# Block-sparse attention and a gated feed-forward on one core: attention values with queries on the output partitions, a ones column in V, batch 0 turned on TensorE, and a list-scheduled program order

## The chip, the cores and the metric

The kernel runs on one core of one Trainium2 chip. The metric is device time in microseconds (us) of one execution. Engines are called as in the profile: PE is TensorE (PEld its weight loads), DVE is VectorE, ACT is ScalarE, POOL is GpSimd, SP is SyncE (SPq, POOLq: their queues, which issue DMAs).

The profile records one execution. Its span, from first to last instruction, is given beside the times: 389.4 us for the kernel before, whose median time is 386.9 us. That profiled run was the slowest of its four (389.81 us), so about 3 us of any difference in spans to it are its own.

## The reference, cut to what matters

```
q, k, v: (4, 8, 768, 64) float32        # batch, heads, sequence, head width
scores = q @ k^T / 8, masked by blocks of 32: neighbours, first and last
         block row and column, and 3 sampled blocks per block row
attn   = softmax(scores);  a = attn @ v
x      = a as (3072, 512)               # 4*768 tokens, 8*64 features
out    = (sigmoid(x @ w_gate) * (x @ w_val)) @ w_out    # 512 -> 1536 -> 512
```

All the work is dense: the kernel computes every score and multiplies the exponentials by a 0/1 mask.

## The kernel before: the parts that matter

Scores are made transposed, with keys on the partitions and queries along the free dimension. A *unit* is one score tile: 256 keys by 256 queries for a pair of heads. There are 144 units, three to a *pair* (256 queries of two heads over all 768 keys), so 48 pairs. Values then have V as the stationary operand. The row sums come from extra matmuls with a block of ones; their reciprocals are spread over the partitions by another matmul.

```
def values(n, p):                       # cut
    t = ps.tile([128, 512], f32, tag="pvz", bufs=1)
    for j in range(NJ):                 # 6 key blocks of 128
        for hd in range(2):
            nc.tensor.matmul(t[hd*64 : hd*64+64, 0:CH], v_[:, hd, j, :],
                pts[j//2][:, hd, (j%2)*CH : (j%2+1)*CH], ...)      # 64 weight columns, 256 wide
    for j in range(NJ):
        for half in range(2):
            for hd in range(2):
                nc.tensor.matmul(t[r0 : r0+32, CH : CH+128], ones, ...)   # row sums, 24 of them
def recips(n, p):  nc.vector.reciprocal(rz, pvz[n, p][:, CH : CH+128])    # 128x128
def unnorm(n, p):  nc.scalar.copy(xu, pvz.pop((n, p))[:, 0:CH])
def spread(n, p):  # two matmuls sel x rz -> rb (PSUM)
def norm(n, p):    nc.vector.tensor_tensor(xT[g, p][...], xu, rb, op=ALU.mult)
```

The order is written by hand. Queries and keys of batch 0 are turned by DMA, and one loop issues two units a step; the feed-forward of a group of 512 tokens begins 16 steps after its attention.

```
for p in range(NP):
    cast_qk(0, p)                       # f32 -> f16 on DVE and ACT
    transpose_qk(0, p)                  # nc.sync.dma_start_transpose
    ...
for s in range(last + 1):
    mine = units[2*s : 2*s+2]
    fi = s - 12 - LAG                   # LAG = 4
    for u in mine: scores(*u)
    if pv_now: values(*pv_now)
    if g is not None: ffn_in(g, f, wg, pgs)
    ... exps, masks, recips, tanhs, unnorm, ffn_in(g, f, wv, pvs), gates, spread, norm, ffn_out
```

The weights are loaded by POOL's queue with a cast to f16, and they are issued from 4.2 us on, right after V of batch 0.

The softmax here doesn't subtract the row's maximum and nothing guards it: scores larger than these inputs give would overflow.

## Time and profile before

| | before |
|---|---|
| median time | 386.89 us (4 runs, 386.20 to 389.81) |
| span of the profiled run | 389.4 us |
| first score matmul | 36.2 us |
| first feed-forward matmul | 94.7 us |
| last matmul ends | 385.5 us |
| PE busy, 0–62 us | 17.4 us |
| PE busy, 150–300 us | 144.4 us, at granted clock 1.00 |

These lines are from the profile page of the kernel before: busy time of the engines; then the span in 40 slices, PE's busy share and the granted clock, in tenths; then the chain of work that ended last, by engine and by line.

```profile
PE 321.1 (82%) x3284; PEld 161.7 (42%) x3284; DVE 226.9 (58%) x359; ACT 197.9 (51%) x269; POOL 40.8 (10%) x53
...
PE   2002277678999999999999999999999999999975
...
PEclk9999996857999999999999999999999999999999
...
PE 68%; ACT 13%; DMA 8%; DVE 4%; issue 4%; SPq 3%; ACTq 0%
PE gv L290 25%; PE py L317 16%; PE pvz L222 11%; ACT pt L203 8%; PE st L192 8%; PE pvz L235 6%; DMA kT<-k_153 4%; DMA ks<-in_k_dram 4%; ACT tg L301 3%; DVE rz L251 2%; SPq L114 2%; PE rb L263 2%; ACT xu L256 1%; DVE y L327 1%; SPq L85 1%
```

PE is the bound from slice 11 on, but it is mostly idle in the first five slices (49 us), and the clock drops in slices 7 to 10. The timeline shows what the start waits for (start us, duration us, queue or engine, line, operation, what it writes and reads):

```profile
20.57 5.05 SPq L114 DMA_TRANSPOSE kT<-k_133  x1
25.71 4.74 SPq L114 DMA_TRANSPOSE qT<-q_151  x1
30.54 4.80 SPq L114 DMA_TRANSPOSE kT<-k_153  x1
...
36.16 1.04 PE L192 MATMUL st<-qT,kT 64*128 64x256 f16 x8 [28.05 <-DMA kT<-k_133]
...
48.26 1.37 SPq L114 DMA_TRANSPOSE kT<-k_169  x1
```

The bracket is PE's idle time before the first scores and what ended it: a DMA transpose that was issued at 20.57 us and landed at 36.1 us.

The next lines are the steady part, in PE's timeline. Each line starts before the one ahead of it has ended, so what one line costs is the distance from its start to the next start.

```profile
206.17 0.61 PE L192 MATMUL st<-qT,kT 64*128 64x256 f16 x8
206.71 0.85 PE L222 MATMUL pvz<-pt,v_1183 128*64 128x256 f16 x12
207.49 0.52 PE L235 MATMUL pvz<-pt,ones 128*32 128x128 f16 x24
207.94 0.39 PE L290 MATMUL gv<-x_1712,wg 128*128 128x512 f16 x1
```

Twelve value matmuls cost 0.78 us and 24 ones matmuls 0.45 us, so 1.23 us a pair. These are the groups that the change removes (count, busy us, mean ns of one, idle before):

```profile
L251 DVE RECIPROCAL rz<-pvz 128x128 f16<-128x128 f32 x48 | 45.7, 952 | 8.1 <-PE pvz L235 8.0
L235 PE MATMUL pvz<-pt,ones 128*32 128x128 f16 x1152 | 27.0, 234 | 0.0
...
L263 PE MATMUL rb<-rz,sel 128*128 128x128 f16 x96 | 13.4, 221 | 9.4 <-ACT tg L301 8.5
```

**A yardstick used throughout: the PE time that a kernel needs.** It is each matmul's count times its spacing at full clock, read from the timelines, plus 0.1 us for each change into or out of the scores' 64-row mode. The last point is where the trace agrees with the Trainium skill, "TensorEngine Tiling (Array Packing)", Key Properties, which says that a change of tiling mode drains TensorE: the last 512-wide matmul before scores is followed after 0.312 us instead of 0.2155 us. For the kernel before:

| part | count x spacing | us |
|---|---|---|
| feed-forward, 512 wide | 864 x 0.2155 | 186.2 |
| scores | 576 x 0.0538 | 31.0 |
| values | 576 x 0.065 | 37.4 |
| ones | 1152 x 0.01875 | 21.6 |
| spreads | 96 x 0.056 | 5.4 |
| block mask | | 2.1 |
| mode changes | 144 x 0.1 | 14.4 |
| sum | | 298.1 |

The span less this sum, 91 us, is called *idle* below. It contains waits, the time before the first and after the last matmul, and what a lower granted clock costs.

### The profile page before, as it was taken

Reading aid. Unit: us, or ns where it says so; the run is one execution under the profiler, and the core shown is the slowest. Engines: PE = TensorE matmul, PEld = TensorE weight load, DVE = VectorE, ACT = ScalarE, POOL = GpSimd, SP = SyncE. Lnnn points to the kernel's source line nnn. Section 1 sums busy time; section 2 is a strip of 40 time slices with the busy share of each in tenths; the row PEclk is TensorE's granted clock in tenths of the full one; section 3 lists DMA queues with packets and bytes.
Section 4 is the critical chain, followed back from the end, with each engine's and each line's share of the span. In section 5 each row is a group of like instructions: output and inputs, shape, how many; then the busy total and the mean of one; then the engine's idle time right before and its main releaser. Section 6 shows DMA issues by size and latency. Waiting matters only on the chain.

```text
span 389.4 us, 7801 instructions
## 1 busy us (share of the span) xinstructions
PE 321.1 (82%) x3284; PEld 161.7 (42%) x3284; DVE 226.9 (58%) x359; ACT 197.9 (51%) x269; POOL 40.8 (10%) x53
## 2 busy tenths in 40 slices
PE   2002277678999999999999999999999999999975
PEld 0001044444555544454444444444444454444432
DVE  5100366677887766767676667676667666432321
ACT  1111256776777766665666566656666564222200
POOL 7200022213220001102020201000000000000000
PEclk9999996857999999999999999999999999999999
DMA  8999988665770003223442450400000000010012
GB/s 186 271 169 195 195 187 194 139 177 85 149 135 2 2 3 108 50 42 112 90 119 51 134 145 12 57 29 29 6 25 27 29 2 29 28 54 29 28 54 81
DMA packets 47151, 33.64 MB, mean 86 GB/s; under 512 B 26996, under 2 KB 44044, under 8 KB 47116
## 3 DMA queue, kind: packets, MB, share of 16 engines
q1 hardware_dynamic: 38012, 25.28, 25.0%
q0 software_dynamic: 9104, 7.87, 14.1%
q8 instruction: 25, 0.41, 0.5%
q14 instruction: 10, 0.08, 0.1%
HBM read 28.42 MB, written 6.29 MB: 89 GB/s over the span
## 4 chain that ended last, share of the span: by engine, by line
PE 68%; ACT 13%; DMA 8%; DVE 4%; issue 4%; SPq 3%; ACTq 0%
PE gv L290 25%; PE py L317 16%; PE pvz L222 11%; ACT pt L203 8%; PE st L192 8%; PE pvz L235 6%; DMA kT<-k_153 4%; DMA ks<-in_k_dram 4%; ACT tg L301 3%; DVE rz L251 2%; SPq L114 2%; PE rb L263 2%; ACT xu L256 1%; DVE y L327 1%; SPq L85 1%
## 5 line engine op out<-in xcount | busy, mean ns | idle before, releaser
L203 ACT ACTIVATE pt<-st 128x1024 f16<-128x1024 f32 x144 | 139.3, 1024 | 83.9 <-PE st L192 83.8
L209 DVE TENSOR_TENSOR pt<-pt,mask 128x1024 f16<-128x1024 f16 x144 | 99.1, 688 | 91.4 <-ACT pt L203 91.4
L192 PE MATMUL st<-qT,kT 64*128 64x256 f16 x576 | 49.5, 292 | 39.0 <-DMA kT<-k_133 28.0
L301 ACT ACTIVATE tg<-gv 128x512 f32<-128x512 f32 x72 | 43.1, 599 | 51.5 <-PE gv L290 49.5
L192 PEld LDWEIGHTS <-kT 64*128 64x128 f16 x576 | 23.7, 98 | 67.0 <-issue 29.1
L251 DVE RECIPROCAL rz<-pvz 128x128 f16<-128x128 f32 x48 | 45.7, 952 | 8.1 <-PE pvz L235 8.0
L290 PEld LDWEIGHTS <-wv 128*128 128x128 f16 x288 | 28.2, 98 | 34.3 <-issue 0.5
L290 PEld LDWEIGHTS <-wg 128*128 128x128 f16 x288 | 23.8, 98 | 29.1 <-issue 4.0
L235 PE MATMUL pvz<-pt,ones 128*32 128x128 f16 x1152 | 27.0, 234 | 0.0
L256 ACT COPY xu<-pvz 128x256 f32<-128x256 f32 x48 | 17.7, 368 | 15.8 <-DVE rz L251 15.7
L327 DVE TENSOR_SCALAR y<-py 128x512 f32<-128x512 f32 x24 | 16.6, 691 | 11.8 <-PE py L317 11.4
L235 PEld LDWEIGHTS <-ones 128*32 128x32 f16 x1152 | 18.0, 102 | 10.9 <-issue 10.9
L263 PE MATMUL rb<-rz,sel 128*128 128x128 f16 x96 | 13.4, 221 | 9.4 <-ACT tg L301 8.5
L263 PEld LDWEIGHTS <-sel 128*128 128x128 f16 x96 | 8.8, 97 | 24.3 <-issue 19.4
L171 PE MATMUL pm<-mb_125,e_70 24*128 24x256 f16 x18 | 4.8, 401 | 4.8 <-DVE mask L178 3.8
L178 DVE CAST mask<-pm 128x512 f16<-128x512 f32 x9 | 5.9, 687 | 0.2
L106 POOL CAST q_2129<-qs 128x768 f16<-128x768 f32 x1 | 0.8, 822 | 43.2 <-issue 43.2
L171 PEld LDWEIGHTS <-e_70 24*128 24x128 f16 x18 | 2.1, 125 | 7.7 <-issue 7.1
L222 PE MATMUL pvz<-pt,v_82 128*64 128x256 f16 x36 | 3.8, 358 | 1.8 <-ACT xu L256 1.8
L104 ACT CAST k_133<-ks 128x768 f16<-128x768 f32 x1 | 0.8, 832 | 8.6 <-DMA ks<-in_k_dram 8.6
L290 PE MATMUL gv<-x_354,wg 128*128 128x512 f16 x12 | 4.6, 386 | 0.5 <-DVE h_1325 L306 0.2
L290 PE MATMUL gv<-x_952,wg 128*128 128x512 f16 x12 | 4.7, 389 | 0.1
(385 smaller groups left out, 540.5 us busy)
## 6 DMA issues: line engine op xcount, KB each, us to landing
qs<-in_q_dram SPq DMA_DIRECT2D x16, 384.0 KB, 3.8
ks<-in_k_dram SPq DMA_DIRECT2D x16, 384.0 KB, 5.2
out_dram<-y SPq DMA_DIRECT2D x24, 256.0 KB, 2.0
wg<-in_moe_w_gate_dram POOLq DMA_DIRECT2D x3, 512.0 KB, 22.8
wv<-in_moe_w_val_dram POOLq DMA_DIRECT2D x3, 512.0 KB, 25.4
wo<-in_moe_w_out_dram POOLq DMA_DIRECT2D x3, 512.0 KB, 30.2
v_76<-in_v_dram POOLq DMA_DIRECT2D x1, 192.0 KB, 3.7
v_82<-in_v_dram POOLq DMA_DIRECT2D x1, 192.0 KB, 6.8
```

The lines of the kernel that those rows point to most:

```text
L192: nc.tensor.matmul(st[:, hd, jj * CH : (jj + 1) * CH], kT[r, j, :], qT[r, 2 * c : 2 * c + 2, :], start=True, stop=True,)
L203: nc.scalar.activation(pt, sts.pop((n, p, tt)), AF.Exp, scale=SCALE)
L209: nc.vector.tensor_tensor(pt, pt, m.unsqueeze(1).to_broadcast([128, 2, 512]), op=ALU.mult)
L222: nc.tensor.matmul(t[hd * 64 : hd * 64 + 64, 0:CH], v_[:, hd, j, :], pts[j // 2][:, hd, (j % 2) * CH : (j % 2 + 1) * CH], start=(j == 0), ...
L235: nc.tensor.matmul(t[r0 : r0 + 32, CH : CH + 128], ones, pts[j // 2][:, hd, o : o + 128], start=False, stop=(j == NJ - 1), skip_group_chec ...
L251: nc.vector.reciprocal(rz, pvz[n, p][:, CH : CH + 128])
L256: nc.scalar.copy(xu, pvz.pop((n, p))[:, 0:CH])
L263: nc.tensor.matmul(rb[:, half * 128 : half * 128 + 128], sel[:, half, :], rz, start=True, stop=True,)
L290: nc.tensor.matmul(t, w[:, i, f * 128 : (f + 1) * 128], xT[g, i], start=(i == 0), stop=(i == NP - 1),)
L301: nc.scalar.activation(t, pgs.pop((g, f)), AF.Tanh, scale=0.5)
L317: nc.tensor.matmul(pys[g, tt], hts[g, f][:, tt * 128 : (tt + 1) * 128], wo[:, f], start=(f == 0), stop=(f == NF - 1),)
L327: nc.vector.tensor_scalar_mul(y, pys.pop((g, tt)), 0.5)
```

## The change

The intent: let the exponentials be the stationary operand, so that queries land on the output partitions; give V a 65th column of ones, so that row sums come with the values; normalise with a per-partition reciprocal; turn the result back with two PE transposes. Batch 0's q and k are turned on PE too. All instructions are described to a small list scheduler with fixed durations, and the program is emitted in the order that it finds. The diff, cut to its core:

```
-            nc.tensor.matmul(t[hd*64 : hd*64+64, 0:CH], v_[:, hd, j, :], pts[...], ...)
-            nc.tensor.matmul(t[r0 : r0+32, CH : CH+128], ones, pts[...], ...)
+        def values():
+            for jq in range(2):
+                for hd in range(2):
+                    for j in range(NJ):
+                        nc.tensor.matmul(
+                            o()[:, 2 * jq + hd, 0:65],
+                            pts[j // 2]()[:, hd, j % 2, jq * 128 : jq * 128 + 128],
+                            v_[:, hd, j, 0:65], start=(j == 0), stop=(j == NJ - 1))
+        P.op("PE", 1.1, values, reads=[*pts, v16[b, p]], writes=[o], prio=seq + 0.1, mode="full")
+        P.op("DVE", 0.15, lambda: nc.vector.reciprocal(rz(), o()[:, :, 64:65]), ...)
+        P.op("DVE", 0.42, ... x16 = o[:, :, 0:64] * rz ...)
+        P.op("PE", 0.12, turn, ...)          # 2 x nc.tensor.transpose, in the same PSUM bank o
+        P.op("ACT", 0.39, ... copy to xT ...)
...
+    def turn_pe(nm, b, p, prio, eng, out_eng):   # batch 0: 6 transposes, then a copy
...
+GROUPS = [[0], [1, 2], [3, 4], [5, 6], [7, 8], [9, 10], [11]]   # feed-forward groups, 256 rows each entry
+LAT = {"PE": 0.35, "ACT": 0.2, "DVE": 0.2, "POOL": 0.25, "SP": 0.1}
+class Plan: ...                               # list scheduler: op(eng, dur, fn, reads, writes, prio)
+    P.run()
-    for s in range(last + 1): ...             # the hand-written order
```

V is now loaded as f32 and cast on POOL (its rows are 66 wide). The weights are loaded in more pieces, and the scheduler places them on POOL's queue after the third cast of V.

## The prediction

> **What bounds it now.** TensorE, after a slow start. By the stretches: 0–62 us has only 17.4 us of PE work, 62–90 us runs at granted clock 0.68, and 150–300 us is 96% busy at clock 1.00. In the timeline the first scores start at 36.2 us (batch 0's eight DMA transposes are issued one behind the other; the chain of waits shows ks, two issues of 4.7 us, then kT 15.6 us), and the feed-forward (FFN) starts only near 98 us, 16 steps later. After that three steps take 13.06 us. The last matmul ends at 385.5 of 389.4 us.
>
> **PE time needed, by pitches in the timeline at full clock** (512-wide matmul 0.2155 us, two score units 0.43 us plus about 0.2 us of row-mode switches, twelve PV matmuls 0.78, 24 ones matmuls 0.45, two spreads 0.11): FFN 864 x 0.2155 = 186; scores 72 x 0.63 = 45; values and ones 48 x 1.23 = 59; spreads 5; masks 3. Sum 298 us.
>
> **Removed:** ones, spreads, the 128x128 reciprocals (952 ns x48), the fp32 copy on ACT (17.7 us), batch 0's DMA transposes.
> **Added:** 24 value matmuls per head pair, 65 columns wide, each with a 128-column weight load; two transposes; a 0.4 us ACT copy; 48 TensorE transposes for batch 0; V casts on POOL.
> The new values depend on weight loads. The Trainium skill ("TensorE: Matmul & The Clock Gate", LDWEIGHTS) gives columns/1.2 ns, 107 ns for 128, but about half with fast weight load. The trace agrees that 128 columns can go faster: the spreads follow each other at 0.055 us, each with its own load. I estimate 46 ns (1.1 us per pair), not over 60 (1.45 us). After: 186 + 45 + 53 + turns 6 + start-up transposes 5 + masks 3 = 298 us. **The PE total does not fall.** The DVE saving (about 35–40 us) and ACT (unchanged, about 200 us) lie off the path.
>
> **What is gained is idle PE time.** Scores should start near 8 us instead of 36, and FFN as soon as weights land. Reads: 3.1 MB of q,k and 1.6 MB of v, then 9.4 MB of weights; at the 200–270 GB/s of the page's early slices the gate/value weights are complete near 42 us (estimate; 40–52). Until then attention runs (ACT and the single o bank hold it to about 1.25 us a unit), some 21 us of PE work plus some 12 of FFN and start-up; then PE is dense: 42 + 265 left + 4% stalls (10) + 4 tail = 321.
>
> **Predicted: 322 us**, range 308 to 342. Faster by over 2%: 0.97; within: 0.02; slower: 0.01.
>
> **What would show it.** First score at 7–10 us; FFN group 0 beginning at 25–40 us; PE about 95% busy from 45 us on; values at 1.1 us a pair; FFN pitch unchanged; DVE near 195 us; so almost all of the gain falls before 100 us, and a few us in the steady state (0.47 us waits for a gv bank vanish).
>
> **What would make it wrong.** Values at 60 ns or over (+17 us); weights later than 52 us; a low clock in the attention-only stretch; the static order, planned with fixed durations (exp 0.93 us where the trace has 0.97 to 1.02), meeting waits on in-order engines: one o bank shared by values and turn, two gv banks; POOL's casts holding back later batches; the 256-wide last group bound by latency (+5 us).

## The result, and the profile after

| | before | after |
|---|---|---|
| median time (4 runs each) | 386.89 us | 321.12 us (319.05 to 322.38) |
| ratio | | 0.8279, 95% interval 0.8232 to 0.8327 |
| span of the profiled run | 389.4 | 320.6 |
| first score / first feed-forward matmul | 36.2 / 94.7 us | 11.7 / 36.9 us |
| PE time needed | 298.1 | 282.1 |
| idle (span less needed) | 91 | 38 |

Ratios are the mean time of one kernel's fast runs over that of the other's fast runs of the same rounds, so they are not quite the ratio of the medians quoted. A control of the changed kernel in a later session (`after_again`) gave 322.13 us and 0.8355.

The total was predicted to within 1 us. The profile shows that two of its terms were not. First the page of the changed kernel, the same rows as before:

```profile
PE 299.2 (93%) x2852; PEld 160.1 (50%) x2852; DVE 204.1 (64%) x374; ACT 196.2 (61%) x279; POOL 51.8 (16%) x69
...
PE   1888898989999999999999999999999999999994
...
PEclk9995999999999999999999999999999999999999
...
PE 69%; ACT 5%; DVE 3%; issue 1%; DVEq 0%; ACTq 0%
PE gv L525 33%; PE py L556 19%; PE o L476 8%; PE st L444 7%; ACT pt L454 4%; PE o L500 1%; DVE h L545 1%; ACT tg L540 1%; DVE pt L462 1%; DVE y L568 1%; DVE x L487 0%; ACT x L505 0%; DVE rz L484 0%; DVEq L545 0%; ACTq L540 0%
```

PE is busy from the second slice on. DMA and SPq have left the chain. The clock was at half once, for 7 us from 24.4 us on; in the control it was not, and the first feed-forward came 2 us earlier there. Then the start, in the timeline:

```profile
9.47 0.82 PE L317 MATMUL gv<-ident,k 128*128 128x128 f16 x6 [2.70 <-POOL k L305]
...
11.71 0.61 PE L444 MATMUL st<-qT,kT 64*128 64x256 f16 x4
...
17.78 0.87 POOL L362 DMA_DIRECT2D wg<-in_moe_w_gate_dram  x1
19.42 0.74 POOL L362 DMA_DIRECT2D wv<-in_moe_w_val_dram  x1
...
35.54 0.45 ACT L505 COPY x<-o 128x256 f16<-128x256 f16 x1
...
36.88 0.60 PE L525 MATMUL gv<-x,wg 128*128 128x256 f16 x4
```

Two things are to be seen. The first scores were ready earlier: their last operand, qT, was copied by 7.8 us. They stand in the fixed order behind the transposes of the *second* k, which waited 2.7 us for POOL's cast, and behind the block mask's first matmuls. And the first weights landed at 21.8 and 24.4 us, but the feed-forward began at 36.9 us, 0.9 us after the end of the copy that completes the first 256 rows of x, behind one more group of value matmuls. It waited for attention, not for weights.

The steady part, in PE's timeline:

```profile
209.74 0.93 PE L476 MATMUL o<-v,pt 128*128 128x65 f16 x24
210.50 1.02 PE L556 MATMUL py<-wo,h 128*128 128x512 f16 x4
211.36 1.03 PE L525 MATMUL gv<-x,wv 128*128 128x512 f16 x4
212.23 0.28 PE L500 MATMUL o<-ident,x 128*128 128x128 f16 x2
212.34 1.03 PE L525 MATMUL gv<-x,wg 128*128 128x512 f16 x4
```

The 24 value matmuls cost 0.76 us from start to next start, not the predicted 1.1 us, which is also the figure that the scheduler was given. The two turns cost 0.11 us. The groups that took the place of those removed:

```profile
L476 PE MATMUL o<-v,pt 128*128 128x65 f16 x1152 | 45.2, 194 | 0.0
...
L487 DVE TENSOR_TENSOR x<-o,rz 128x256 f16<-128x256 f32 x48 | 20.4, 424 | 1.7
...
L484 DVE RECIPROCAL rz<-o 128x4 f32<-128x4 f32 x48 | 8.5, 177 | 10.6 <-PE o L476 10.2
L500 PE MATMUL o<-ident,x 128*128 128x128 f16 x96 | 13.6, 224 | 1.0 <-DVE x L487 1.0
```

PE time needed is therefore 186.2 (feed-forward) + 31.0 (scores) + 35.9 (values, 1152 x 0.0312) + 5.4 (turns) + 2.7 (batch 0's transposes) + 2.1 (masks) + 18.8 (188 mode changes) = 282.1 us, 16 us less than before; the prediction had 298.

The tail is held as feared: the last group is 256 wide, and its gate and value matmuls follow at 1.18 us a step where their PE time is 8 x 0.1078 = 0.86 us:

```profile
306.30 0.60 PE L525 MATMUL gv<-x,wv 128*128 128x256 f16 x4
306.74 0.60 PE L525 MATMUL gv<-x,wg 128*128 128x256 f16 x4
307.48 0.60 PE L525 MATMUL gv<-x,wv 128*128 128x256 f16 x4
```

### The profile page after: what moved, and what is told of

The parts are those of the page before. It is cut to its first block, busy times and chain, and to the rows that moved or that the text cites. A ratio compares the mean times of both kernels' runs of the same rounds, so it can differ in the third digit from the quotient of the medians.

```text
span 320.6 us, 6860 instructions
## 1 busy us (share of the span) xinstructions
PE 299.2 (93%) x2852; PEld 160.1 (50%) x2852; DVE 204.1 (64%) x374; ACT 196.2 (61%) x279; POOL 51.8 (16%) x69
## 4 chain that ended last, share of the span: by engine, by line
PE 69%; ACT 5%; DVE 3%; issue 1%; DVEq 0%; ACTq 0%
PE gv L525 33%; PE py L556 19%; PE o L476 8%; PE st L444 7%; ACT pt L454 4%; PE o L500 1%; DVE h L545 1%; ACT tg L540 1%; DVE pt L462 1%; DVE y L568 1%; DVE x L487 0%; ACT x L505 0%; DVE rz L484 0%; DVEq L545 0%; ACTq L540 0%
## 5 line engine op out<-in xcount | busy, mean ns | idle before, releaser
L454 ACT ACTIVATE pt<-st 128x1024 f16<-128x1024 f32 x144 | 143.1, 1040 | 43.5 <-PE st L444 42.7
L462 DVE TENSOR_TENSOR pt<-pt,mask 128x1024 f16<-128x1024 f16 x144 | 105.7, 744 | 33.5 <-ACT pt L454 33.0
L540 ACT ACTIVATE tg<-gv 128x512 f32<-128x512 f32 (+1 forms) x84 | 46.2, 550 | 59.7 <-PE gv L525 56.1
L525 PE MATMUL gv<-x,wv 128*128 128x512 f16 (+1 forms) x336 | 76.1, 349 | 2.5 <-DVE h L545 1.5
L525 PE MATMUL gv<-x,wg 128*128 128x512 f16 (+1 forms) x336 | 76.2, 349 | 0.7 <-ACT tg L540 0.4
L545 DVE SCALAR_TENSOR_TENSOR h<-tg,gv 128x512 f16<-128x512 f32 (+1 forms) x84 | 51.0, 607 | 38.7 <-PE gv L525 36.1
L556 PE MATMUL py<-wo,h 128*128 128x512 f16 x288 | 70.4, 379 | 0.8 <-DVE y L568 0.8
L476 PEld LDWEIGHTS <-pt 128*128 128x128 f16 x1152 | 41.7, 98 | 10.6 <-issue 4.2
L525 PEld LDWEIGHTS <-wv 128*128 128x128 f16 x336 | 30.3, 97 | 32.7 <-issue 10.6
L476 PE MATMUL o<-v,pt 128*128 128x65 f16 x1152 | 45.2, 194 | 0.0
L556 PEld LDWEIGHTS <-h 128*128 128x128 f16 x288 | 26.1, 98 | 28.4 <-issue 3.4
L505 ACT COPY x<-o 128x256 f16<-128x256 f16 x48 | 18.6, 388 | 8.6 <-PE o L500 8.5
L487 DVE TENSOR_TENSOR x<-o,rz 128x256 f16<-128x256 f32 x48 | 20.4, 424 | 1.7
L305 POOL CAST q<-qs 128x768 f16<-128x768 f32 x15 | 14.5, 969 | 10.6 <-DMA qT<-q 7.3
L484 DVE RECIPROCAL rz<-o 128x4 f32<-128x4 f32 x48 | 8.5, 177 | 10.6 <-PE o L476 10.2
## 6 DMA issues: line engine op xcount, KB each, us to landing
wg<-in_moe_w_gate_dram POOLq DMA_DIRECT2D x2, 512.0 KB, 10.3
```

Source lines behind the costliest of these rows:

```text
L305: lambda: f(c(), s().rearrange("p h j d -> p j h d")),
L454: lambda st=st, pt=pt: nc.scalar.activation(pt().rearrange("p h j q -> p h (j q)"), st(), AF.Exp, scale=SCALE),
L462: nc.vector.tensor_tensor(t, t, mask()[:, c, tt].unsqueeze(1).to_broadcast([128, 2, 512]), op=ALU.mult)
L476: nc.tensor.matmul(o()[:, 2 * jq + hd, 0:65], pts[j // 2]()[:, hd, j % 2, jq * 128 : jq * 128 + 128], v_[:, hd, j, 0:65], start=(j == 0), ...
L487: lambda: nc.vector.tensor_tensor(x16().rearrange("p j (h d) -> p (j h) d", d=64), o()[:, :, 0:64], rz().to_broadcast([128, 4, 64]), op=AL ...
L505: lambda: nc.scalar.copy(dst()[:, i * CH : (i + 1) * CH], tT().rearrange("p j q -> p (j q)")),
```

## The experiments

Twelve runs were made beside those of the two kernels. They fell in three sessions on three chips: `a_` and `b_oldvalues`; `b_dma0`, `c_width`, `c_nomask` and `c_wlate`; and the rest. Only the last has a control of the changed kernel, and the two measurements of that kernel differ by 0.9% in their ratios (0.8279 and 0.8355), so differences of 2 to 5 us to it are small beside what a session can add. "Span" and "idle" are of the profiled run; idle is the span less the needed PE time, computed as above for each kernel.

| run | what it is | median us | ratio to before | first score / feed-forward, us | needed / idle, us |
|---|---|---|---|---|---|
| before | | 386.9 | | 36.2 / 94.7 | 298 / 91 |
| `a_values` | hand order, new values | 357.0 | 0.9245 | 21.7 / 80.8 | 275 / 82 |
| `a_turn` | hand order, batch 0 on PE | 372.5 | 0.9672 | 24.2 / 74.4 | 301 / 68 |
| `a_both` | hand order, both | 338.2 | 0.8767 | 18.5 / 61.3 | 278 / 59 |
| after | all three parts | 321.1 | 0.8279 | 11.7 / 36.9 | 282 / 38 |
| `after_again` | control | 322.1 | 0.8355 | 11.4 / 34.9 | 282 / 36 |
| `b_oldvalues` | plan, old values | 363.1 | 0.9426 | 10.6 / 43.5 | 302 / 60 |
| `b_dma0` | plan, batch 0 by DMA | 326.7 | 0.8430 | 16.7 / 40.5 | 278 / 47 |
| `x_vsplit` | before, V loads split | 384.4 | 0.9961 | 32.5 / 92.4 | 298 / 89 |
| `c_nomask` | plan, no mask multiplications | 318.6 | 0.8229 | 11.2 / 34.3 | 282 / 35 |
| `c_wlate` | plan, weights later | 317.2 | 0.8206 | 10.3 / 33.7 | 281 / 33 |
| `c_halfexp` | plan, early exponentials halved | 317.5 | 0.8210 | 10.2 / 33.5 | 282 / 33 |
| `d_best` | plan, three mends | 339.4 | 0.8766 | 8.0 / 37.9 | 280 / 58 |

`c_width` is left out of the table: a look at one spacing, one run.

### The three parts one by one

**`a_values`: the new values alone, in the hand order.** V's rows became 66 wide, which a single load could not fill, so each V load was split by head. The last two lines of the cut tell the edit in words.

```
-    t = work.tile([128, 2, NJ, 64], f16, tag="v16", bufs=8)
-    nc.gpsimd.dma_start(t, vv[b][:, 2*p : 2*p+2])
+    t = vring[(b*NP + p) % 8]                      # 66 wide, ones in column 64
+    for h in range(2):
+        nc.gpsimd.dma_start(t[:, h, :, 0:64], vv[b][:, 2*p + h])
-    values, ones, reciprocal 128x128, copy, spread, multiply
+    24 value matmuls, reciprocal 128x4, multiply; next step: 2 transposes into gv, ACT copy
```

> The kernel before in its hand order, with the new value matmuls, normalisation and turn alone. In the changed kernel's timeline 24 value matmuls take 0.77 us where before the values and ones took 1.23 us, 48 times. Theory A (the new values save about 22 us of TensorE time, against the recorded prediction that TensorE's total does not fall): 364 to 374 us. Theory B (the recorded one: no saving of TensorE time): 380 to 390 us.

Measured: 357.0 us, more than theory A asked. The needed PE time fell by 23 us. But the first score also came 14.5 us earlier; with this form of the V loads the first weights landed only at 29.5 us instead of 18.1 us, which is the likely reason (see `x_vsplit`; not shown). How much of that start is in the gain? After 12 units the run is 5.3 us ahead (54.6 against 59.9 us), at the first feed-forward matmul 13.9 us, at the last score 31.3 us. So at most about 5 us of the 32 us in span are the start's. The 17.4 us from the first feed-forward to the last score fit the values: 38 pairs x 0.46 us = 17.5. Of the 8.6 us between, eight pairs explain 3.7; the other 5 (an estimate) go with the granted clock, which was 0.67 there before and 0.95 in this run. The statement that the PE total does not fall is refuted.

**`a_turn`: batch 0 turned on PE alone, in the hand order.**

```
+            if b == 0:
+                g = ps.tile([128, NJ, 128], f16, tag="gv", bufs=2)
+                for j in range(NJ):
+                    nc.tensor.transpose(g[:, j, :], c[:, j]..., ident16)
+                (nc.scalar.copy if nm == "k" else nc.vector.tensor_copy)(t, g)
+                continue
             nc.sync.dma_start_transpose(t, ...)
```

> The kernel before in its hand order, batch 0 turned on TensorE alone. First score near 14 us instead of 36, held by loads that share the DMA with the weights; the steady part unchanged (three steps 13.06 us). Theory A (start is worth what it is early by): 362 to 370 us. Theory B (the start only moves a wait to the later loads of batch 0 or to the weights): over 378 us.

Measured: 372.5 us, between the two theories. The first score came at 24.2 us, not 14: the hand order puts all eight turns, each with its load and cast, before the first score. The 12 us won at the start arrived nearly whole at the end (12.7 us by the ratio: (1 − 0.9672) x 386.2). (The profiled run is 20 us ahead of that of the kernel before, in span and at the first feed-forward; some of that is the slow profiled run of the latter, named at the beginning, and its low clock.)

**`a_both`: both, so that the program order (and what comes with it) is what remains.** The edit is the two above together.

> Hand order with both the new values and batch 0 turned on TensorE, so that it differs from the changed kernel by the list-scheduled order (and how V is cast). If the two gains add: 342 to 352 us, and the order is worth the 21 to 31 us that remain to 321. If the order is worth nothing: 321 us.

Measured: 338.2 us, a little better than the expectation of added gains (the two ratios give 29.2 + 12.7 = 41.9 us; together they give 47.6 us); why it is more than the sum was not separated. The remaining 17 us to the changed kernel are the list-scheduled order and what belongs to it: finer weight loads that come later, V cast on POOL, batch 0's casts spread over three engines, uneven groups. In that step the needed PE time rises by 4 us (188 mode changes instead of 144) and idle falls by 20 us; the first feed-forward comes at 36.9 instead of 61.3 us.

**`b_oldvalues`: the old values put back into the plan.** Values, ones, reciprocal, copy, spread and multiply as before, with durations 1.23, 0.95, 0.37, 0.12 and 0.42 us. The planner got stuck at first, because a spread held a gv bank while it waited for a buffer of x; x is therefore reserved at the spread.

```
-        P.op("PE", 1.1, values, ...)      # 24 matmuls, 65 wide
+        P.op("PE", 1.23, values, ...)     # 12 + 24 ones, into the one bank o
+        P.op("PE", 0.12, turn, reads=[rz, sel], writes=[rb, dst], ...)   # rb in the gv banks
```

> The changed kernel with the old values, ones, 128x128 reciprocals and spreads put back in the plan. Theory A (the new values save TensorE time): 335 to 346 us. Theory B (recorded: TensorE's total does not fall with them): 319 to 326 us.

Measured: 363.1 us, worse than either theory. It needs 20 us more of PE, as theory A says; another 21 us is idle, and 17 of these lie between 50 and 100 us, where PE is busy 37.9 of 50 us (47.8 in the changed kernel) and the granted clock is 0.85. There the planner emits a dozen score units in a row, with no feed-forward between them, so that PE waits for each exponential. That is a poor order that it found for *this* program, partly through my reservation of x. The run agrees in sign with theory A, but it does not size the values.

**`b_dma0`: batch 0 back to DMA transposes, in the plan's order.**

```
-            turn_pe(nm, 0, p, -40 + i, ...)
+            turn_dma(nm, 0, p, -40 + i, {"k": "ACT", "q": "DVE"}[nm] if p == 0 else "POOL")
```

> The changed kernel with batch 0 turned by DMA transposes again, in the plan's order. The first score goes back from 11.7 us to 25 to 36 us, and the weights, which share the DMA with the transposes, end later. If the start is worth what it is early by: 338 to 348 us. If feed-forward work fills the hole: under 328 us (not expected, since it needs attention first).

Measured: 326.7 us. My expectation missed. The first score came 5 us later, at 16.7 us, not 13 to 24 us later, and the time grew by 5 us (3 to 6 by the ratios). The reason is in SP's timeline of this run:

```profile
10.39 3.14 SPq L329 DMA_TRANSPOSE qT<-q  x1
13.63 1.23 SPq L329 DMA_TRANSPOSE kT<-k  x1
14.96 1.23 SPq L329 DMA_TRANSPOSE qT<-q  x1
```

The last two issues take 1.23 us each, and these transposes landed 3.7 and 3.0 us after their issue. In the kernel before, the same instruction took 4.7 to 5.1 us to issue between 20 and 35 us and landed 15 us later, and again 1.37 us at 48.26 us, when the last weights had landed at 48.2 us. In `b_dma0` the first weight load is issued at 20.9 us. The slow start before was thus not the price of a DMA transpose alone, but of one beside other loads. The weights are the likely ones, but not the only possible ones: the first two transposes of `b_dma0` took 2.8 and 3.1 us to issue (the second is the first line above; it landed after 6.2 us) beside loads of q, k and v alone, and one issued beside the weights, at 21.95 us, took 1.24 us and landed after 6.9 us. How many transfers already wait in the queue may matter as much; that was not separated.

**`x_vsplit`: an attempt to show that by the order of the loads alone.**

```
-        nc.gpsimd.dma_start(t, vv[b][:, 2*p : 2*p+2])
+        for h in range(2):
+            nc.gpsimd.dma_start(t[:, h], vv[b][:, 2*p + h])
```

> The kernel before with each V load of the GpSimd queue split in two, nothing else. In the run with the new values in hand order the same split (needed for V's new row width) put the weight loads 5 to 11 us later and the first score at 21.7 us instead of 36.2. Theory: batch 0's DMA transposes are slow because the weights share the DMA with them, so this alone starts the scores near 22 to 26 us and takes 370 to 378 us. Rival: the transposes themselves are slow, or the start does not count: 384 to 388 us.

Measured: 384.4 us, ratio 0.9961 with an interval of 0.9897 to 1.0025: the same. It says little about the theory, because it did not do what it was made for: the weights were issued 1.3 us later, and the first landed at 18.2 us (before 18.1 us), the last 2 us earlier than before. The transposes stayed slow (most 4.5 to 5.9 us to issue, some 16 us to landing) and the first score came 3.6 us earlier. What it does show is that splitting the loads is not by itself what helped `a_values`. That weights delay the transposes rests on the issue times in three traces, not on a run that moved the weights alone.

### What sets the spacing of the value matmuls

**`c_width`: the second to sixth matmul of each group narrowed to 65, 49, 33 and 17 columns** (wrong result).

```
-                            o()[:, 2 * jq + hd, 0:65], ... v_[:, hd, j, 0:65]
+                            o()[:, 2 * jq + hd, 0:w], ... v_[:, hd, j, 0:w]
+            # w = 65 if j == 0 else (65, 49, 33, 17)[2 * jq + hd]
```

> The changed kernel with the second to sixth value matmul of each group 65, 49, 33 and 17 columns wide in the four groups (wrong result on purpose). It measures what sets their pitch of about 31 ns. If the 128-column weight load sets it, the pitch stays at 31 ns for all widths. If the moved columns set it, it falls with the width: 49 columns to about 24, 17 columns to 10 or to a floor.

Measured, from start to next start in the records after 32 us: 33 ns between matmuls that are 65 wide, and 25 ns (median) between those that are 49, 33 and 17 wide alike. So neither theory is whole. There is a floor of 25 ns for these matmuls, which use the whole array (the scores, on half of its rows, start in twos 3 ns apart), and below some width the moved columns no longer matter. At 65 columns the moved columns set the spacing, and the 128-column weight load, which each of the matmuls has, is hidden in no more than 25 ns. The prediction's 46 ns took the weight load to be the limit.

### What holds the start

**`c_wlate`: the weights later.**

```
+    gate_w = P.op("POOL", 0.1, lambda: nc.gpsimd.tensor_copy(late(), tr["q", 0, 3]()[:, 0, 0:16]),
+                  reads=[tr["q", 0, 3]], writes=[late], after=[gate_w], prio=-21)
```

> The changed kernel with the weight loads issued about 4.5 us later (they wait on GpSimd for the last turned q of batch 0), so that the gate and value weights are complete near 43 us instead of 38.8. Theory W (recorded: feed-forward starts as soon as weights land, TensorE starves until then): 4 to 5 us slower, 325 to 327 us. Theory X (the first feed-forward waits for the attention of its 256 rows, done at 36 us, when its weights have lain there for 12 us): within 1.5 us of 321.

Measured: 317.2 us with a correct result, 4 to 5 us *faster* than the changed kernel. The weights did come later: the first landed at 25.4 us (21.8 in the changed kernel, 22.6 in the control), gate and value weights were complete at 41.2 us (38.8 and 37.3). The feed-forward began at 33.7 us, again 0.9 us after the end of the copy that completes x:

```profile
32.41 0.44 ACT L510 COPY x<-o 128x256 f16<-128x256 f16 x1
...
33.74 0.60 PE L530 MATMUL gv<-x,wg 128*128 128x256 f16 x4
```

Theory W is refuted; theory X is right about what the feed-forward waits for, though the time fell further than its 1.5 us. Why it is faster is not settled, and its session had no control of the changed kernel: the last V cast of batch 0 now comes before the weight issues, the whole order shifted, and idle fell by 3 to 5 us in small pieces. It is the fastest correct kernel.

**`c_nomask`: no mask multiplications** (wrong result; the operation stays in the plan and emits nothing).

> The changed kernel without the mask multiplications on VectorE (wrong result on purpose), program order unchanged: 105.7 us of VectorE work less. In the changed kernel VectorE is 90% busy and over from 20 to 52 us. Theory D (VectorE holds the early attention): feed-forward starts 4 to 7 us earlier than 36.8 us and the time falls by 4 to 8 us. Theory E (ScalarE's exponentials or the order itself hold it): less than 2 us.

Measured: 318.6 us, 2.6 to 3.6 us less, between the theories, for 106 us of DVE work taken away. The first feed-forward came 2.6 us earlier than in the changed kernel and 0.6 us earlier than in the control. From 30 to 52 us DVE is busy for only 7.0 of 22 us here, yet PE does no more than in the control (19.3 us, control 19.5) and ACT stays full (21.2 us). DVE is at most a small part of what holds the start.

**`c_halfexp`: exponentials and masks of the second and third 256 queries at half width** (wrong result).

```
-  nc.scalar.activation(pt[...], st(), AF.Exp, scale=SCALE)
+  nc.scalar.activation(pt[...][:, :, 0:w], st()[:, :, 0:w], AF.Exp, scale=SCALE)   # w = 256 if n in (1, 2) else 512
   (masks the same; values read the first half twice)
```

> The changed kernel with the exponentials (and masks) of the second and third blocks of 256 queries at half width (wrong result on purpose), program order unchanged: about 10 us of ScalarE work less, all between 25 and 60 us. If ScalarE holds the early attention, as its full busy time from 30 to 52 us suggests: 312 to 317 us. If the o bank's round trip or the weights hold it: 319 us or more.

Measured: 317.5 us, 3.7 to 4.7 us less, just above the range expected if ScalarE holds the start. These are busy times from 30 to 52 us (PE, PEld, DVE, ACT, POOL, then granted clock, DMA share, GB/s), first of the control, then of this run:

```profile
30.00:52.00 22.00, 19.47 (x281) 12.88 (x278) 20.46 (x40) 21.02 (x31) 3.70 (x4) 1.00 1.17 264
```

```profile
30.00:52.00 22.00, 21.82 (x331) 15.68 (x329) 16.91 (x45) 15.25 (x35) 4.77 (x6) 1.00 1.20 269
```

ACT is 96% busy in the control. With less work on it, PE goes from 19.5 to 21.8 of 22 us and takes over as the bound. DVE lost work as well here; `c_nomask`, where it lost far more and the time fell less, is why I put the effect down mostly to ACT. So until about 52 us the start is held by ScalarE's exponentials (about 1 us a unit, plus the copies of x), and PE has little else to do until the first x is complete.

### An attempt to do better

**`d_best`**: weights as in `c_wlate`, plus three mends.

```
-GROUPS = [[0], [1, 2], ..., [9, 10], [11]]
+GROUPS = [[0], [1], [2, 3], ..., [10, 11]]
-    p24 = psb("st", [128, 1024])
+    p24, p24b = psb("py", [128, 512]), psb("o", [128, 256])
-    dma=1.22 / P.op("PE", 1.1, values / "ACT", 0.93 (exp)
+    dma=3.2 for k of pair 1, else 1.22 / 0.78 / 0.97
```

> Three mends in the changed kernel: the plan is told durations nearer the measured ones (values 0.78 us, exponentials 0.97 us, the third load 2 us later), so that the first score comes before the second pair's transposes; the block mask no longer goes through a score bank; the last group is 512 rows wide, so that the last feed-forward is not held by the wait from matmul to activation; and weights as in the run with later weights. First score 8 to 9 us, last matmul to end as before: 311 to 317 us. If the start and the tail are filled by other waits: 318 to 322 us.

Measured: 339.4 us, 17 to 18 us worse than the changed kernel and outside both expectations. The first score did come at 8.0 us. Everything after it was worse. The same columns as above, for the control and then for this run:

```profile
42.00:62.00 20.00, 18.50 (x248) 12.94 (x246) 14.77 (x31) 13.95 (x25) 8.77 (x10) 1.00 1.15 289
90.00:115.00 25.00, 25.00 (x265) 13.38 (x262) 19.07 (x35) 20.85 (x30) 10.09 (x10) 1.00 0.86 197
```

```profile
42.00:62.00 20.00, 14.85 (x158) 9.16 (x157) 15.16 (x27) 15.86 (x21) 6.34 (x6) 0.75 1.17 276
90.00:115.00 25.00, 19.73 (x200) 12.13 (x197) 17.15 (x30) 18.95 (x25) 11.20 (x10) 0.80 0.94 240
```

PE ran dry twice, and both times the granted clock fell; over the run it was at half for 32 us, against 1 us in the control. Needed PE time is nearly the same (280 us), idle is 58 us instead of 36. Which of the mends did it (the groups, the durations or the banks of the block mask) was not separated and stays open.

## Why the prediction was right, and what in it was wrong

The time (322 predicted, 321.1 measured) and the direction were right, and so was the main reading: PE is the bound, and the gain at the start is PE's idle time. That the number is within 1 us is luck, though: it was a sum of three terms, and they missed by amounts that cancel.

| term | predicted | measured |
|---|---|---|
| PE work done by 42 us | 33 (idle 9) | 22 (idle 20) |
| PE work left after 42 us | 265 | 260 |
| stalls and tail after 42 us | 14 | 18 |
| total PE work | 298 | 282 |
| sum: 42 + left + stalls and tail | 321 | 320.6 (span) |

1. **"PE total does not fall": wrong.** The step was "I estimate 46 ns" for a value matmul. It measured 32 ns; `c_width` shows that a narrower matmul with the same weight load goes down to 25 ns, so the load was not the limit. `a_values` and `a_both` show the effect in the hand order: 23 us less PE time needed, and 29 us less time in `a_values`, of which up to 5 us belong to its earlier start and about 5 to a higher granted clock (an estimate, see there). Nor is the cheaper streaming the whole of it: of the 0.46 us saved on each pair, about 0.2 us (some 9 us in all) are the two changes of array width in the old values and ones, which the new form does not have. The prediction counted them as part of the old spacing without seeing them. In the changed kernel the added mode changes (4.4 us) and batch 0's transposes (2.7 us) reduce it to 16 us.
2. **"FFN as soon as weights land": wrong.** It started when the first 256 rows of x were complete, 12 us after the first weights. `c_wlate` delayed the weights and cost nothing. What the prediction named beside it, that ACT holds attention in this stretch, was right, and `c_halfexp` supports it. The early attention advanced at about 1.15 us a unit (36 exponentials from 12.4 to 54 us), near the 1.25 predicted. But the PE work in it is smaller than assumed, since values are cheap and those of only six pairs were done by 42 us (27 units of scores, so nine pairs, were); and the 12 us put down for feed-forward and start-up were 7 by 42 us.
3. **"First score at 7–10 us": late, at 11.7 us.** The planner expected the second k earlier than it came, and PE stood still behind it. `d_best`, which told the planner so and moved the block mask to other banks, put the score first and got 8.0 us.
4. **"Almost all of the gain falls before 100 us": too strong.** Of the 69 us in span, 44 us are idle time that vanished before 100 us, 9 us idle time after it (mostly in the steady part), and 16 us are less PE work, most of it after 100 us. Not all of the vanished idle time was waiting: the kernel before ran at half clock for 24 us between 59 and 93 us, the changed one for 7 us and its control not at all before the end. At most half of the 24 us, 12 us, can be lost to that (an estimate); how much was, no run separates. The prediction named the low clock of that stretch but gave it no term.
5. **Right as predicted:** the bound (PE after a slow start); the unchanged 0.2155 us per feed-forward matmul; DVE at 204 us (195 predicted); the 0.47 us waits of the spreads gone; the last group bound by latency (0.32 us a step, at most 4 us in its twelve steps, where the prediction said 5). PE's 95% was reached from 62 us on rather than 45 (from 42 to 62 us it was 90%).

Of the three parts of the change, in the hand order the new values gave 29 us (with up to 5 us of start and about 5 of clock), PE turning of batch 0 gave 13 us, both 48 us, and the list-scheduled order with its loads another 17 us. Undone in the plan's order, PE turning is worth about 5 us. What the values are worth there could not be sized, since `b_oldvalues` was spoiled by a poor order.

## What to carry to other kernels

Write down the needed time of the bounding engine and the idle time as two separate numbers, and check each against the trace: a right total can hide a cheap operation and a late start that cancel. Before a late start is charged to the operation that is slow there, look for the same operation elsewhere in the trace: the DMA transposes took 5 us to issue in a crowded start, with the weight loads in flight, and 1.2 us later on, and in the order that issues the weights after most of them, replacing them was worth about 5 us instead of 13. A list-scheduled static order is worth having (17 us here) but is brittle: changes of its inputs moved the time by −5 and by +17 us, so each new plan has to be measured.

## What the Trainium skill lacked or had wrong

- "TensorE: Matmul & The Clock Gate", LDWEIGHTS (loading the stationary operand): columns/1.2 ns, which is 107 ns for 128 columns, and, under Weight-path perf modes, "~2× (measured)" for fast weight load. Here each value matmul has its own 128-column load, and they follow each other at 32 ns (65 wide) and at 25 ns (49 wide and less), so the load costs at most 25 ns of spacing. The records of the loads themselves do not size it: they last 98 ns on average here, and 102 ns for the 32-column loads of the old ones. The same page's floor of about 25 ns from start to start (Wait — 56ns, not 53.3ns?) agrees with `c_width`.
- The same page, Back-to-back issue gap, gives a sustained 131 ns for 512-wide matmuls with their weight loads. In these traces they follow each other at 0.2155 us, which is that section's isolated figure of about 216 ns; 128-wide ones follow at 56 ns, not at 81 ns.
- "TensorEngine Tiling (Array Packing)", Key Properties, says that a change of tiling mode drains TensorE, but not what it costs: about 0.1 us each way here (0.312 us instead of 0.2155 us before scores), 14 to 19 us in the whole kernel for the scores' mode. Changes between 64, 32 and 128 columns cost as much: about 0.1 us for each of 96 in the kernel before.
- No page gives a size for a DMA transpose beside large loads ("DMA: Bandwidth & Descriptors" would be the place): issue 1.2 us and about 3 us to landing where little else was in flight; 4.7 to 5.1 us and 15 us in the kernel before, with the weights in flight; 3.1 us and 6.2 us beside loads of q, k and v in `b_dma0`. What sets it was not separated.
